# Folding the tokens on VectorE behind the transpose instead of on TensorE before it, in a kernel of linear attention and a gated long convolution

## The chip, the cores and the metric

The kernel runs on one core of one Trainium2 chip. The metric is the device time of one execution in microseconds (us). PE is TensorE, DVE is VectorE, ACT is ScalarE, POOL is GpSimd and SP is SyncE, which here only issues DMAs.

## The reference, cut to what matters

```python
r = np.maximum(x, 0);  phi(x) = concat([r * cos(theta_s), r * sin(theta_s)])   # theta_s = pi/2 * s / S
kv  = einsum('bhsf,bhsd->bhfd', phi(k), v);   z = sum_s phi(k)
att = einsum('bhsf,bhfd->bhsd', phi(q), kv) / (einsum('bhsf,bhf->bhs', phi(q), z) + 1e-6)
x   = att.transpose(0, 2, 1, 3).reshape(8, 576, 512)
x1, x2, x3 = split(x @ w_proj, 3)                     # w_proj is 512 x 1536
x2_conv = irfft(rfft(x2, axis=1) * rfft(filter, axis=0), n=576, axis=1)
out = (x1 * x2_conv * x3) @ w_out                     # float32, 8 x 576 x 512
```

There are 8 batches, 8 heads, 576 tokens and a head size of 64.

## The kernel before, in words

Everything on the chip is in fp16 but for the sums, which TensorE leaves in PSUM as fp32. A batch goes through these steps; the short names are those of the order written out by hand at L886 to L972.

- `Lq`, `Lk`, `Lv` (L147): GpSimd issues loads that turn fp32 into fp16. The first 512 tokens lie four to a row in 128 rows, the last 64 in the lower half of a fifth tile. Each load is two DMAs.
- `pk` (L499): ten operations make relu(k) times cosine and times sine for the five tiles. `pq` (L513): six make relu(q) and relu(q) times tangent. `va` (L533): copies v.
- `kv` (L549): 40 matmuls of 65 columns. `qt` (L566): q is transposed, for batches 0 and 1 on PE, from batch 2 on by four DMA transposes that SP issues (L570, `DMA_QT = 2`). `num` (L593): 40 matmuls of 65 columns, and on DVE a sum, a reciprocal and a multiplication that write `att`, the attention, with tokens in the partitions.
- `fx` (L622): for each of four blocks of channels, four matmuls of 144 columns (L627) and two of 160 (L633) multiply `att` by tables of a few cosines. They transpose it and fold the 576 tokens, by the symmetries of the transform, in one go. ACT brings the result into SBUF.
- `xt` (L652): one DMA transpose of the whole of `att` (20 blocks of 128 by 128) feeds the gates; batch 0 does it on PE (`xp`).
- `pr` (L669): the folded tokens times the middle third of `w_proj`, 16 matmuls of 512 columns and four that fill 64 of the 128 output rows.
- `dft` (L694): 24 matmuls with 32 stationary columns each, 16 of 512 and 8 of 128 moving columns, in three PSUM units; then on DVE products with the filter's spectrum (L712 to L722).
- `ga`, `gb` (L725): 64 matmuls of 288 columns (L731) make x1 and x3 with channels in the partitions, ACT evicts, and `g` multiplies them.
- `inv` (L755): 24 matmuls back to tokens. `y` (L774): per block of channels two operations undo one fold, two the other, and two multiply by `g`; the last one also gathers the 64 left tokens.
- `out` (L807): 16 matmuls of 512 columns and 8 of 256, an eviction, and stores.

PSUM holds four units of two banks, handed out in turn. Helpers record most DVE operations under two lines: L112 (`tsc`, a tensor and a scalar) and L117 (`tt`, two tensors); ACT evictions stand under L137 (`ev`). Every engine works its own list strictly in the order of the plan, so several batches are interleaved by hand and a waiting instruction holds up all that stands behind it.

Of the kernel before, what the change touches and what calls it, by code (L numbers as in the profile page):

```python
# [13 lines left out]
I32 = mybir.dt.int32  # L14


@with_exitstack
def kernel(
# [17 lines left out]


# [11 lines left out]


# [7 lines left out]
    FX = 65536.0  # L58
    SP_ = NJ * 128
    NM = NC * 128  # L60

    consts = ctx.enter_context(tc.tile_pool(name="consts", bufs=1))
    work = ctx.enter_context(tc.tile_pool(name="work", bufs=1))
    psum = ctx.enter_context(tc.tile_pool(name="psum", bufs=4, space=bass.MemoryType.PSUM))
    setup_stack = ExitStack()
    setupp = setup_stack.enter_context(tc.tile_pool(name="setupp", bufs=1))
    late = {}

    def unit(name):
        return psum.tile([128, 2, 512], FP32, tag="u", bufs=4, name=name)  # L70

    def const(name, shape, dt=FP32):
        return consts.tile(shape, dt, tag=name, name=name)

    ccol = const("ccol", [128, NJ])
    scol = const("scol", [128, NJ])
    tcol = const("tcol", [128, NJ])
    epsc = const("epsc", [128, NJ])
    ident = const("ident", [128, 128], FP16)
    half_pi = const("half_pi", [128, 1])  # L80
    m_half_pi = const("m_half_pi", [128, 1])
    m_pi = const("m_pi", [128, 1])
    m_half = const("m_half", [128, 1])
    wr_col = const("wr_col", [128, 1])
    fm = const("fm", [128, 9, 16], FP16)
    fme = const("fme", [128, 4, 5, 16], FP16)
    fcos = const("fcos", [128, 288], FP16)
    fsin = const("fsin", [128, 288], FP16)
    itab = const("itab", [128, 6, QS], FP16)
    itl = const("itl", [128, NC, 2, 2, QS], FP16)  # L90
    hE = const("hE", [128, 2, DM], FP16)
    hO = const("hO", [128, 2, DM], FP16)
    hL = const("hL", [128, 3, 128], FP16)
    wp16 = const("wp16", [128, NC, 3 * DM], FP16)
    wo16 = const("wo16", [128, NC, DM], FP16)
    warm = setupp.tile([128, 512], FP16, tag="warm", name="warm")
    filt16 = setupp.tile([NP, 2, 3 * DM], FP16, tag="filt16", name="filt16")
    feo = setupp.tile([NP, 2, 3, DM], FP16, tag="feo", name="feo")
    k32, v32 = (
        work.tile([128, 4, NJ * D], FP32, tag="att", bufs=2, name=f"{x}32") for x in "kv"  # L100
    )
    qpt_buf = const("qpt", [128, NH, SP_], FP16)
    va_buf = [const(f"va{i}", [128, NH, NJ, 66], FP16) for i in range(2)]
    raw_buf = [const(f"raw{i}", [128, NH, NJ * D], FP16) for i in range(6)]

    last_dve = [None]

# [14 lines left out]
    def rnd(out, in0, mul, add):  # L122

        tsc(out, in0, mul, AL.mult, add, AL.add)
        tsc(out, out, RC, AL.add, -RC, AL.add)

    cc = {}
    mark = {}

    which = [""]  # L130
# [8 lines left out]
    raw_t = {}  # L139
    DMA_QT = 2  # L140
    HALF = (slice(0, 4), slice(4, 8), slice(0, 8))
    held = [None]

    def at(half):
        return HALF[half]

    def load_rows(queue, rw, src, b, hs):  # L147
        to = slice(0, rw.shape[1]) if rw.shape[1] < NH else hs
        first = queue.dma_start(  # L149
            out=rw[:, to, 0 : 4 * D],  # L150
            in_=src[b, hs, 0:NM].rearrange("h (p j) d -> p h (j d)", j=4),
        )
        if held[0] is not None:
            tc.add_manual_dep(
                first.ins, held[0].ins.name,
                mybir.DependencyInfo(mybir.DependencyClass.Sync, mybir.DependencyReason.DATA),
                reason="hold",
            )
        queue.dma_start(
            out=rw[0:64, to, 4 * D : 5 * D], in_=src[b, hs, NM:S].rearrange("h p d -> p h d")  # L160
        )

    def step_load(nm):
        def load(b, half):
            raw_t[(b, nm)] = raw_buf[(3 * b + "qkv".index(nm)) % len(raw_buf)]
            load_rows(nc.gpsimd, raw_t[(b, nm)], {"q": q, "k": k, "v": v}[nm], b, at(half))
            yield
        return load
# [7 lines left out]
    def step_wp(w):  # L176
        nc.gpsimd.dma_start(
            out=wp16[:, :, ds(w * DM, DM)],
            in_=moe_w_proj.rearrange("(i p) n -> p i n", p=128)[:, :, ds(w * DM, DM)],
        )  # L180

        yield

    def step_filt():
        for x in range(2):
            nc.gpsimd.dma_start(
                out=filt16[:, x],
                in_=moe_filter_fft[ds(x * HS, HS)].rearrange("(p j) n -> p (j n)", j=3),
            )
            yield  # L190

    def step_wo():
        nc.gpsimd.dma_start(out=wo16, in_=moe_w_out.rearrange("(i p) n -> p i n", p=128))
        yield

# [5 lines left out]
    def step_iota(part):  # L201
        if part == 0:
            iota("s4_i", [128, NJ], lambda t: [
                (t[:, 0:4], [[1, 4]], 0, 4), (t[0:64, 4:5], [[1, 1]], NM, 1),
                (t[64:128, 4:5], [[1, 1]], 0, 1),
            ])
            yield
            return
        if part == 1:
            iota("p_i", [128, 1], lambda t: [(t, [[1, 1]], 0, 1)])  # L210
            iota("kr_i", [128, 4, 2], lambda t: [(t, [[1, 4], [0, 2]], 1, 0)])
            iota("nrow_i", [128, 128], lambda t: [(t, [[1, 128]], 0, 0)])
            iota("er_i", [128, 4, 16], lambda t: [(t, [[1, 4], [4, 16]], 0, 0)])
            yield
            return
        iota("fr_i", [128, 320], lambda t: [
            (t[:, 0:32], [[9, 2], [18, 16]], 0, 0),
            (t[:, 0:1], [[1, 1]], HS, 0),
            (t[:, 32:160], [[2, 2], [-8, 2], [18, 32]], 10 - HS, 0),
            (t[:, 160:288], [[2, 2], [10, 2], [18, 32]], 1 - HS, 0),  # L220
            (t[:, 288:320], [[9, 2], [18, 16]], 0, 0),
        ])
        iota("s3_i", [128, 3], lambda t: [(t, [[1, 3]], 0, 3)])
        iota("sg_i", [128, 32], lambda t: [(t, [[-2, 2], [0, 16]], 1, 0)])
        iota("sr_i", [128, QS], lambda t: [(t, [[2, 2], [8, QS // 2]], 1, 0)])
        yield

    cc["p"], cc["m"] = small("p"), small("m")
# [4 lines left out]

    def step_ones(i):
        nc.vector.memset(va_buf[i][:, :, :, D : D + 2], 1.0 / A1)
        yield

    def step_cols():
        nc.vector.memset(warm, 0.0)
        nc.vector.memset(half_pi, PI / 2.0)  # L240
        for r in (k32, v32):
            nc.vector.memset(r[64:128, :, 4 * D : 5 * D], 0.0)
        yield
# [4 lines left out]
        yield  # L248
        p = cc["p"]
        nc.vector.tensor_copy(out=p, in_=cc["p_i"])  # L250
        yield
        tsc(ident, cc["nrow_i"], p, AL.is_equal)
# [7 lines left out]
        m = cc["m"]  # L260
        rnd(m, p, 1.0 / 16.0, -15.0 / 32.0)
        yield
        lo = small("lo")
        stt(lo, m, -16.0, p)
        yield
        m8 = small("m8")
        tsc(m8, m, 1.0 / 9.0, AL.mult, -8.0 / 9.0, AL.add)
        yield
        ph = small("ph", 8).rearrange("p (k c) -> p k c", c=2)
        tsc(ph, cc["kr_i"], m8, AL.mult)  # L270
        yield
        tsc(ph[:, :, 0], ph[:, :, 0], 0.25, AL.add)
        yield
        rr = small("ph_r", 8).rearrange("p (k c) -> p k c", c=2)
        tsc(rr, ph, RC, AL.add, -RC, AL.add)
        yield
        nc.vector.tensor_tensor(out=ph, in0=ph, in1=rr, op=AL.subtract)
        yield
        coef = small("coef", 9)
        nc.vector.memset(coef[:, 8:9], 1.0)  # L280
        yield
        nc.scalar.activation(
            out=coef[:, 0:8], in_=ph.rearrange("p k c -> p (k c)"), func=AF.Sin, scale=TWO_PI
        )
        yield
        match = small("match", 16)
        tsc(match, cc["nrow_i"][:, 0:16], lo, AL.is_equal)
        yield
        nc.vector.tensor_tensor(
            out=fm,  # L290
            in0=coef.unsqueeze(2).to_broadcast([128, 9, 16]),
            in1=match.unsqueeze(1).to_broadcast([128, 9, 16]),
            op=AL.mult,
        )
        yield
        tsc(fme, cc["er_i"].unsqueeze(2).to_broadcast([128, 4, 5, 16]), p, AL.is_equal)
        yield
        nc.vector.memset(m_half_pi, -PI / 2.0)
        yield
        nc.vector.memset(m_pi, -PI)  # L300
        yield
        nc.vector.memset(m_half, -FX / 2.0)
# [3 lines left out]

# [4 lines left out]
    def sin_of(dst, m):  # L311
        nc.scalar.activation(
# [3 lines left out]
    def cos_of(dst, m):  # L316
        a = setupp.tile([128, 3 * 320], FP32, tag="tg_a", bufs=1, name="tg_a")
        nr, nc_ = dst.shape
        a = a[0:nr, 0:nc_]
# [6 lines left out]
    def step_rows():  # L326

        p, m = cc["p"], cc["m"]
        sgn = cc["sgn"] = setupp.tile([NP, 32], FP32, tag="sgn", name="sgn")
        nc.vector.tensor_copy(out=sgn, in_=cc["sg_i"][0:NP])  # L330
        yield
        kq = small("kq")
        rnd(kq, p, 1.0 / 32.0, -31.0 / 64.0)
        yield
        k2 = small("k2")
        rnd(k2, kq, 0.5, -0.25)
# [470 lines left out]
    def step_out(b, grp, cut=0):  # L807
# [4 lines left out]
        for cs in ((range(NC),), (range(NC - 1), range(NC - 1, NC)))[cut]:  # L812
            for x, t in enumerate(tiles):
# [14 lines left out]
                if cut and t < 4 and cs[0] > 0:  # L828
                    yield
# [175 lines left out]
```

## Time and profile before

| | |
|---|---|
| runs | 242.19, 251.63, 245.29 us; median 245.29 |
| profiled execution, span | 242.5 us |
| mean granted clock of TensorE | 0.961 |

The page of the profiled execution cuts the span into 40 equal slices of 6.06 us. A digit is the busy share of an engine in tenths, and PEclk the granted clock in tenths.

```profile
PE   6077988978999799998859985999999999999990
DVE  5999878995898998949946985499969967949760
ACT  4259998894888587766617790578768877866741
PEclk9679999997999999999979997999999999999998
DMA  6999999989999999999999999959999933260244
```

All engines start early; DVE is full from the second slice, PE from the fourth. PE falls to 5 to 8 in slices 19 to 25, and the clock shows a dip three times after the start. The DMA engines are taken up until late.

### The profile page before, as it was taken

The numbers are of one execution on the slowest core, as the hardware profiler recorded it, in microseconds if no ns is written. First come the engines' busy times: TensorE is split into PE (matmuls) and PEld (weight loads), VectorE is DVE, ScalarE is ACT, GpSimd is POOL, SyncE is SP. The second block draws the span as 40 slices with busy tenths as digits, with TensorE's granted clock in tenths as the row PEclk, the third lists the DMA queues.
The fourth block names the chain that finished last, engine by engine and source line by source line (L and its number), as shares of the span: only waits on it lengthen the run. The fifth ranks groups of instructions, "written<-read, shape, count | busy, mean of one in ns | idle before, by whom it ended". The sixth has DMA issues, their size and how long they took to land.

```text
span 242.5 us, 5900 instructions
## 1 busy us (share of the span) xinstructions
PE 210.4 (87%) x2276; PEld 142.2 (59%) x2276; DVE 193.1 (80%) x657; ACT 168.6 (70%) x268; POOL 46.4 (19%) x75
## 2 busy tenths in 40 slices
PE   6077988978999799998859985999999999999990
PEld 2066776455558467764527653685678567846740
DVE  5999878995898998949946985499969967949760
ACT  4259998894888587766617790578768877866741
POOL 8882252003331042200220070000200000000000
PEclk9679999997999999999979997999999999999998
DMA  6999999989999999999999999959999933260244
GB/s 170 184 187 201 199 197 190 110 132 194 163 174 164 201 145 209 209 194 219 164 186 189 160 186 211 181 118 242 122 140 192 184 108 124 84 122 1 88 151 151
DMA packets 95612, 39.70 MB, mean 164 GB/s; under 512 B 63648, under 2 KB 91296, under 8 KB 95584
## 3 DMA queue, kind: packets, MB, share of 16 engines
q0 software_dynamic: 38464, 16.26, 54.8%
q1 hardware_dynamic: 56752, 22.49, 46.7%
q10 hardware_dynamic: 368, 0.59, 0.7%
q8 instruction: 17, 0.28, 0.5%
q14 instruction: 11, 0.09, 0.1%
HBM read 33.69 MB, written 9.44 MB: 178 GB/s over the span
## 4 chain that ended last, share of the span: by engine, by line
PE 57%; DVE 16%; DMA 14%; ACT 6%; SPq 3%; issue 2%; ACTq 0%; DVEq 0%
PE x L731 21%; PE out L816 10%; PE x L673 9%; DMA qpt<-qp 7%; DMA xt<-att 5%; PE num L599 3%; PE inv L760 3%; PE inv L764 3%; DVE qp L112 3%; DVE att L117 3%; PE kv L556 2%; DVE kp L112 2%; PE fx L627 2%; SPq L570 2%; PE dft L704 2%
## 5 line engine op out<-in xcount | busy, mean ns | idle before, releaser
L731 PE MATMUL x<-xt,wp 128*128 128x288 f16 x512 | 72.3, 289 | 5.0 <-DMA xt<-att 4.3
L731 PEld LDWEIGHTS <-wp 128*128 128x128 f16 x512 | 48.9, 99 | 21.4 <-DMA xt<-att 5.4
L673 PE MATMUL x<-wp,fx 128*128 128x512 f16 (+1 forms) x160 | 34.5, 387 | 0.0
L816 PE MATMUL out<-wo,y 128*128 128x512 f16 x128 | 31.6, 394 | 0.0
L137 ACT CAST x0s<-x 128x576 f16<-128x576 f32 x32 | 20.4, 641 | 13.9 <-PE x L731 12.4
L137 ACT ACTIVATE os<-out 128x1024 f32<-128x1024 f32 (+1 forms) x22 | 17.5, 795 | 17.6 <-PE out L816 15.7
L137 ACT CAST x2s<-x 128x576 f16<-128x576 f32 x32 | 20.4, 642 | 11.2 <-PE x L731 9.8
L117 DVE TENSOR_TENSOR att<-num,rcp 128x640 f16<-128x640 f32 x32 | 25.9, 820 | 0.5
L137 ACT ACTIVATE x2f<-x 128x1024 f16<-128x1024 f32 (+1 forms) x24 | 20.8, 882 | 7.6 <-PE x L673 7.3
L673 PEld LDWEIGHTS <-fx 128*128 128x128 f16 (+1 forms) x160 | 13.5, 101 | 15.6 <-issue 2.4
L117 DVE TENSOR_TENSOR eo<-eq 128x288 f16<-128x288 f16 x64 | 17.4, 297 | 5.4 <-ACT eq L137 5.4
L137 ACT CAST eq<-inv 128x576 f16<-128x576 f32 x32 | 20.1, 649 | 2.0 <-PE inv L764 1.8
L599 PE MATMUL num<-kvs,qpt 128*128 128x65 f16 x320 | 14.8, 198 | 7.2 <-DMA qpt<-qp 6.7
L816 PEld LDWEIGHTS <-y 128*128 128x128 f16 x128 | 12.6, 102 | 13.9 <-issue 2.5
L599 PEld LDWEIGHTS <-qpt 128*128 128x128 f16 x320 | 13.5, 101 | 10.6 <-DMA qpt<-qp 7.3
L149 POOL DMA_DIRECT2D raw<-in_k_dram x8 | 7.0, 878 | 62.7 <-DVE y L117 55.0
L760 PE MATMUL inv<-itab,yf 128*128 128x144 f16 x128 | 18.0, 232 | 0.6 <-DVE yf L117 0.6
L137 ACT CAST fx<-fx 128x576 f16<-128x576 f32 x30 | 18.1, 653 | 0.3 <-PE fx L633 0.2
L137 ACT CAST xf<-dft 128x1024 f16<-128x1024 f32 (+1 forms) x24 | 17.9, 810 | 0.2 <-PE dft L704 0.2
L117 DVE TENSOR_TENSOR y<-eo 128x288 f16<-128x288 f16 x64 | 17.6, 301 | 0.4
L764 PE MATMUL inv<-itl,yf 128*128 128x288 f16 x64 | 17.5, 294 | 0.0
L117 DVE TENSOR_TENSOR yf<-m,m 128x512 f16<-128x512 f16 (+1 forms) x48 | 15.5, 349 | 0.7
(153 smaller groups left out, 375.4 us busy)
## 6 DMA issues: line engine op xcount, KB each, us to landing
out_dram<-os SPq DMA_DIRECT2D x30, 256.0 KB, 4.6
raw<-in_v_dram POOLq DMA_DIRECT2D x7, 512.0 KB, 8.4
raw<-in_q_dram POOLq DMA_DIRECT2D x7, 512.0 KB, 10.0
raw<-in_k_dram POOLq DMA_DIRECT2D x7, 512.0 KB, 8.6
wp<-in_moe_w_proj_dram POOLq DMA_DIRECT2D x3, 512.0 KB, 11.3
out_dram<-os SPq DMA_DIRECT2D x15, 64.0 KB, 2.3
filt<-in_moe_filter_fft_dram POOLq DMA_DIRECT2D x2, 288.0 KB, 13.8
k<-in_k_dram SPq DMA_DIRECT2D x1, 512.0 KB, 3.9
```

The costliest lines, as they stand in the source:

```text
L112: last_dve[0] = nc.vector.tensor_scalar(out=out, in0=in0, scalar1=s1, scalar2=s2, op0=op0, **({"op1": op1} if op1 else {}))
L117: last_dve[0] = nc.vector.tensor_tensor(out=out, in0=in0, in1=in1, op=op)
L137: return nc.scalar.copy(out=out, in_=in_) if mul is None else nc.scalar.mul(out=out, in_=in_, mul=mul)
L149: first = queue.dma_start(out=rw[:, to, 0 : 4 * D], in_=src[b, hs, 0:NM].rearrange("h (p j) d -> p h (j d)", j=4),)
L556: nc.tensor.matmul(u[:, g, ds((h % 4) * 65, 65)], kp[:, j, h].rearrange("p a b -> p (a b)"), va[:, h, j, 0:65], start=(j == 0), stop=(j == ...
L570: nc.sync.dma_start_transpose(out=qpt[:, hsl].rearrange("p h (j n) -> p (h j) n", j=NJ), in_=qp[:, hsl].rearrange("p h j a b -> p (h j a b)"),
L599: nc.tensor.matmul(u[:, hh, ds(t * 65, 65)], qpt_buf[:, h, ds(t * 128, 128)], kvs[:, h // 4, ds((h % 4) * 65, 65)], start=True, stop=True,)
L673: nc.tensor.matmul(dst, fx[:, c, ds(128 * ch, n)], wp16[:, c, ds(DM, DM)], start=(c == cs[0]), stop=(c == cs[-1]),)
L731: nc.tensor.matmul(u[:, hf, 0:HS], wp16[:, i, ds(w * DM + c * 128, 128)], xt[:, i, ds(HS * hf, HS)], start=(i == 0), stop=(i == NC - 1),)
L760: nc.tensor.matmul(u[:, comp, ds(par * QS, QS)], yf[par][:, comp, ds(c * 128, 128)], itab[:, par + 4 * comp], start=(par == 0), stop=False,)
L764: nc.tensor.matmul(u[:, comp, 0:HS], yf[2][:, comp], itl[:, c, comp].rearrange("p a b -> p (a b)"), start=False, stop=True,)
L816: nc.tensor.matmul(u[:, x], y[:, c, ds(QS * t, 128)], wo16[:, c], start=(c == 0), stop=(c == NC - 1),)
```

## The change

The loads deal the tokens nine to a row: row p holds tokens 9p to 9p+4 in the lower 64 partitions and 9p+5 to 9p+8 in the upper 64, with zeros in the upper half of the fifth tile. So the two halves of a tile hold mirrored residues, and the fold becomes an addition and a subtraction of a tile's first half with another's second half read backwards.

`fx` is gone. `bf` takes its place: eight additions and subtractions on DVE, on `xt`, the transposed attention. The DFT is four matmuls with 128 stationary columns (`dm`), four with 64 rows that add the left tokens (`dr`), and 24 with 32 columns and 128 moving ones (`dl`).

```diff
-    DMA_QT = 2
+    DMA_QT = 1
...
+        rows = src[b, hs].rearrange("h (p j) d -> p h (j d)", j=9)
+        first = queue.dma_start(out=rw[0:64, to], in_=rows[:, :, 0 : NJ * D])
...
+        queue.dma_start(out=rw[64:128, to, 0 : 4 * D], in_=rows[:, :, NJ * D : 9 * D])
...
+    def step_bf(b, x):
...
+        for x_, op in ((0, AL.add), (1, AL.subtract)):
+            tt(
+                out=eo_buf[:, cs, x_, 0:256].rearrange("p c (t n) -> p c t n", t=4),
+                in0=a[:, :, :, 0], in1=a[:, :, ::-1, 1, ::-1], op=op,
+            )
+            yield
+        for x_, op in ((0, AL.add), (1, AL.subtract)):
+            tt(
+                out=eo_buf[:, cs, x_, 256:HS], in0=a4[:, :, 0:32], in1=a4[:, :, ::-1][:, :, 0:32],
+                op=op,
+            )
+            yield
...
+    def step_dm(b, bl):
+        u = pu[b, bl] = unit()
+        for comp, tab, cl in ((0, fcos, 2 * bl), (1, fsin, 2 * bl + 1)):
+            nc.tensor.matmul(
+                u[:, comp], tab[:, ds(128 * bl + 32 * comp, 128)], x2f[:, cl],
+                start=True, stop=False,
+            )
+        yield
+
+    def step_dr(b):
+        for bl in range(2):
+            for s_ in range(2):
+                comp = (s_, 1 - s_)[bl]
+                rows = ds(64 * s_, 64)
+                nc.tensor.matmul(
+                    pu[b, bl][:, comp], flo[rows, bl], x2f[rows, 4], start=False, stop=True,
+                )
+        yield
```

The second half of `bf` folds the results once more, again with four operations (main part and left part, sum and difference). Beyond that:

- `pk` makes relu(k) in one operation over all five tiles and relu(k) times tangent in five; the cosine goes onto v instead (`va`, five operations in place of four copies).
- `xt` is two DMA transposes of 10 blocks; `qt` of batch 1 goes by DMA too. Each gate's eight matmuls stand in the plan as two groups of four.
- `y` works on two blocks of channels at a time (one, for the last batch); left tokens are separate small operations, and one multiplication by `g` covers all 576 tokens. `pd` merges the left part of the products with the second main part.
- Buffers are fixed by name, and a string `UNITS` says which of the four PSUM units each use takes.
- The order of every engine's list is new, and more evictions of the first batches go to DVE, while parts of `pk`, `pq` and `va` go to ACT throughout.

By the built lists, PE goes from 2,276 matmuls to 2,140, DVE from 657 operations to 618 and ACT from 270 to 254; SP issues 42 transposes where it issued 31.

## Prediction

> **What bounds the kernel now.** I read the busy times of the page first, then the shares of the chain of waits, then a stretch of that chain in order of time, then the waits and the stages.
>
> ```profile
> PE 210.4 (87%) x2276; PEld 142.2 (59%) x2276; DVE 193.1 (80%) x657; ACT 168.6 (70%) x268; POOL 46.4 (19%) x75
> ...
> PE 57%; DVE 16%; DMA 14%; ACT 6%; SPq 3%; issue 2%; ACTq 0%; DVEq 0%
> ```
>
> PE is the busiest engine and holds over half of the chain, but DVE is only 17 us behind it: whatever moves from PE to DVE soon meets a second bound. The next view is a stretch of the chain in which nothing but PE stands (start, duration, what), and it gives PE's pace, which the busy time hides because matmuls overlap.
>
> ```profile
> 158.45 0.98 PE x L731 x8
> 159.43 0.25 PE fx L627 x4
> 159.68 0.14 PE fx L633 x2
> ...
> 165.23 3.45 PE x L673 x16
> 168.68 0.98 PE x L731 x8
> 169.66 0.55 PE x L673 x4
> 170.22 1.09 PE dft L704 x24
> ```
>
> A matmul of 512 columns costs 216 ns (3.45 / 16), one block of channels of `fx` 0.39 us, a batch's DFT 1.09. Then the waits (engine, line, releaser: total us, times, longest).
>
> ```profile
> PEld L599 <- DMA qpt<-qp: 7.3, 2, 4.0
> ...
> PE num L599 <- DMA qpt<-qp: 6.7, 2, 3.7
> ...
> PE x L731 <- DMA xt<-att: 4.3, 3, 1.8
> ```
>
> The stages: stretch, length, then busy time (and instructions) of PE, its weight loads, DVE, ACT and POOL, granted clock, DMA share, GB/s.
>
> ```profile
> 80.00:100.00 20.00, 18.35 (x202) 11.79 (x201) 18.98 (x66) 13.27 (x21) 6.36 (x8) 1.00 1.26 193
> ...
> 220.00:242.50 22.50, 16.29 (x120) 9.92 (x117) 13.12 (x44) 10.67 (x20) 0.00 (x0) 0.96 0.31 106
> ```
>
> PE loses 11.0 us to transposes that land late (6.7 + 4.3). From 80 to 100 us DVE is busy 18.98 of 20 (95%), the most that it reaches over a long stretch, and in the last 22.5 it leaves 9.4 idle.
>
> **PE, part by part.** `fx` goes: 4 blocks x 0.39 x 8 batches = -12.5 us. The PE transposes of batch 1 go: the chain has ten of them in 0.68, so 4 x 0.68 = -2.7. The DFT grows. `dm` is four matmuls of 512 columns, 0.86. `dr` is four with 64 rows; no row shows whether two in different rows of the array run side by side, so it lies between 0.43 and 0.86; the nearest row, four DFT matmuls in different columns, runs side by side, and I take 0.43. `dl` is six groups of four small ones: in the old 1.09, four groups of 512 columns take 0.86, which leaves 0.11 for each of its two small groups, so 0.66. Together 1.95 to 2.4 against 1.09: +6.9 (to +10.3) over eight batches. `pr`'s left part is two groups of four instead of two pairs, the same 0.55. Gates, `inv`, `out`, `kv` and `num` keep their matmuls. PE's sum is -12.5 - 2.7 + 6.9 = -8.3 (-4.9 at the dear end of `dr`).
>
> [...]
>
> **DVE.** I take busy time over count from the groups, since neighbours overlap: 0.65 us for 1,024 fp16 elements of two tensors (10.4 / 16), 0.40 for 512 (12.8 / 32), 0.45 for 576, 0.27 for 256, 0.20 for 128 (3.2 / 16), and some 0.17 to 0.25 below that.
> - `bf`: batches 1 to 7 have four of 1,024 and four of 128, 3.4 us each; batch 0 does halves, some 4.6. Together +28.4. The backward reads have no row as inputs; `y`'s backward writes cost the 301 ns of its plain neighbours. [...] I take the pace of the writes.
> - `y`: four groups made 56.2 us (17.4 + 17.6 + 13.3 + 7.9). Now a pair costs four of 512, four of 64 and one of 1,152: 3.1, 14 times, and the last batch's singles 2.2 each: 52.2. So -4.
> - `pd`: 41.1 (20.8 + 4.3 + 12.8 + 3.2) becomes 24 of 1,024, 8 of 1,280, 8 of 256, 16 of 512 and 16 of 640: 38. So -3.
> - `pk`, `pq`, `va`: 55.7 us before. What stays on DVE is 40 of 512 elements with `tcol` and 18 with `ccol` at 0.32 to 0.35, 12 of 2,560 at 0.85, and a few halves: 38. So -17.5.
> - Evictions moved over from ACT: some six of 576 elements at 0.75, three of 1,024 and two of 512 (no row; 0.75 scaled by elements, 1.2 and 0.7), the rest small: +10. Fewer table steps: -3.
>
> DVE's sum is 193.1 + 28.4 - 4 - 3 - 17.5 + 10 - 3 = 204.
>
> **ACT.** `fx`'s evictions go (-18.1). Scaled operations arrive: 47 of 512 elements and a few of 256. The nearest rows are 541 ns for 288 elements with a column of scales and 498 for 256, so about 0.73 for 512: +39, less the copies of v and the old `kp` of 13.6. With evictions handed to DVE and PSUM copies of q's transposes that go, some -12, it comes to 164. ACT stays third.
>
> **Which end is late.** PE alone gives 242.5 - 8.3 = 234.2. DVE at 204 with the share that the bounding engine had before (87%) gives 234.5, and its floor is lower: 204 plus the 3.1 and 9.4 idle at the two ends and 5% of the middle makes 227. The two engines become level, so I take 234 and no more.
>
> **Queues and waits.** The fold stands in DVE's list and waits for the landing of the second half of `xt`; behind it stand `pk`, `pq`, the reciprocals of `num` and `pd` of other batches, and who waits for those is PE, through PSUM units. By the built list, the DVE work between the last write of `att` and the first fold is 5.4, 7.9, 4.5, 7.6, 7.5, 8.9 and 3.3 us for batches 1 to 7. The whole `xt` landed in 6.1 (4.9 to 7.5), a `qpt` of 10 blocks in 3.8 (3.4 to 10.1). At 6.1 only batches 1, 3 and 7 are uncovered, 0.7 + 1.6 + 2.8 = 5 us of DVE's idle, which the share above already has room for. On SP 24 + 7 transposes become 28 + 14; their issue took 24 x 1.42 + 7 x 3.23 = 57 us of the span, and four more at 1.42 lie beside all else. POOL's loads move 640 and 512 bytes per piece where they moved 512 and 128, with a third fewer pieces: no cost. The startup has about as much DVE work as before up to the first gate; 2 us either way.
>
> **The rivals.**
> 1. *The folds wait for late transposes (slower).* For: `num` already waited 3.7 us for a transpose while loads ran, and such landings reached 10.1. If every `xt` took 10.1, the uncovered time is 4.7 + 2.2 + 5.6 + 2.5 + 2.6 + 1.2 + 6.8 = 25.6: 260 us. Against: no whole `xt` took over 7.5, which leaves 2.1 + 3.0 + 4.2 = 9.3, or 243. It decides from about 16 us uncovered, 2.3 per batch. The granted clock falls with such a wait, 0.91 between 111 and 129 us, where PE waited 2.99. [...]
> 2. *DVE becomes the bound, with backward reads at half pace.* [...] For: DVE is already full early. Against: backward writes were not slow.
> 3. *The new order also fills the stalls.* Without the 11.0 us of late transposes: 223. For: `xt` in halves lets a gate start on the first. Against: batch 1 now waits for DMA too.
> 4. *`fx` was hidden.* Its matmuls ran where PE would have waited anyway, and the end stays at 242. Against: the chain has them.
>
> **How the numbers follow.** The sum is made against the span of 242.5; the fastest run shown is 0.3 below it, the median 2.8 above, so I put 1 us on 234. Chances: forecast 0.42 (228 to 241), rival 3 0.20, rival 2 0.15, rival 4 0.06, rival 1 0.17. Within 2% of 245.29 (240.4 to 250.2) is about what a measurement can tell from no change. Faster by more: 0.42 + 0.20, less a little for the upper end, 0.61. Within: 0.21. Slower: rival 1 and a tail of 2, 0.18. The range from 222 to 250 holds rivals 2, 3 and 4 and leaves most of rival 1 outside.
>
> **What would show it.** PE: `dft` near 2 us per batch in the chain, no `fx`, busy near 200. DVE near 204, backward folds at 0.65 us and not 1.2. ACT near 164. DVE's waits for `xt` by DMA below 6 us in all. PE and DVE level in the middle stages. I am wrong if DVE is near full while PE has gaps (rival 2), if the folds wait over 16 us for DMA (1), or if PE's waits for `qpt` are gone (3).

## The result, and the profile after

| | before | after |
|---|---|---|
| median of the runs | 243.74 us (241.3 to 251.63, 4 runs) | 394.73 us (393.03 to 395.3, 4 runs) |
| profiled execution, span | 242.5 us | 393.2 us |
| mean granted clock of TensorE | 0.961 | 0.776 |

The ratio is 1.633 (95% interval 1.625 to 1.642); this ratio and those below leave out executions that took over 1.5% longer than the fastest of the same kernel, which the medians keep. The forecast was 235 with a range of 222 to 250: the direction was wrong.

First the page of the kernel after: busy times, the slices (9.8 us each now), and the shares of the chain of waits.

```profile
PE 228.0 (58%) x2140; PEld 141.1 (36%) x2140; DVE 209.9 (53%) x618; ACT 164.5 (42%) x252; POOL 41.5 (11%) x78
...
DMA  8999899999997994999729999199951931111111
...
DMA 35%; SPq 21%; PE 20%; DVE 12%; issue 3%; ACT 3%; POOL 1%; DVEq 0%; ACTq 0%
```

No engine got much more to do, and none is the bound: PE fell from 87% to 58% of the span. PE's 228 us are no more work either, since part of it ran at a granted clock of 0.50 (224 to 251 us, for one), where a gate matmul takes 447 ns against 286 at 1.00. DMA and SP's queue hold 56% of the chain, where they held 17%. The last seven slices show the DMA engines at a tenth: something still runs there, on few of the engines.

Next its waits (engine, line, releaser: total us, times, longest).

```profile
PEld L670 <- DMA qpt<-qp: 64.9, 9, 12.6
PE ps L670 <- DMA qpt<-qp: 61.1, 7, 12.2
...
ACT os L253 <- DMA out_dram<-os: 32.7, 3, 16.2
...
PE ps L837 <- DMA xt<-att: 26.2, 4, 15.5
```

PE waits 87.3 us for transposes (61.1 + 26.2) where it waited 11.0. ACT's line is the one that gives the clue: an eviction waits until a store has freed its buffer, 16.2 us long. The end of the chain says the same (start, duration, what).

```profile
353.39 22.16 DMA out_dram<-os
```

A store of 256 KB took 22.16 us to land. At the 53 GB/s of the next view 256 KB are 5 us of work (an estimate), so it stood behind other stores. Last, two stretches by windows (length, then busy time and count of PE, its weight loads, DVE, ACT and POOL, granted clock, DMA share, GB/s), with PE long done:

```profile
354.00:375.00 21.00, 0.00 (x0) 0.00 (x0) 1.18 (x3) 0.77 (x2) 0.00 (x0) 0.50 0.14 53
375.00:393.00 18.00, 0.00 (x0) 0.00 (x0) 0.42 (x1) 0.38 (x1) 0.00 (x0) 0.50 0.15 54
```

Only stores are in flight there. The DMA share is 0.14 and 2 of 16 is 0.125: about what two of the 16 DMA engines make that are always busy, at 53 GB/s. In the kernel before the last 6.5 us had a share of 0.47 and 156 GB/s.

What the diff changed there is one line of `out` that neither the excerpt of the change nor the prediction speaks of. With tokens dealt nine to a row, a tile holds token j of each row in its lower half and token j + 5 in its upper, and the store follows that:

```diff
-        ov = out[b, 0:NM].rearrange("(i t) n -> t i n", t=4)      # a store: 128 rows of 512
+        rows = out[b].rearrange("(p j) n -> j p n", j=9)
+        ov = [rows[t : t + 6 : 5] for t in range(4)]               # a store: 2 x 64 rows of 512
```

The bytes, the rows of 2 KB and the number of stores are the same; the outermost dimension went from 128 to 2. That a store with an outermost size of 2 runs on two engines was a guess from this size and the share of 0.14 in the window; e1 to e4 were run to try it.

### The profile page after: what moved, and what is told of

Its sections match the earlier page's. It is cut to its first block, busy times and chain, and to the rows that moved or that the text cites. A ratio compares the mean times of both kernels' runs of the same rounds, so it can differ in the third digit from the quotient of the medians.

```text
span 393.2 us, 5622 instructions
## 1 busy us (share of the span) xinstructions
PE 228.0 (58%) x2140; PEld 141.1 (36%) x2140; DVE 209.9 (53%) x618; ACT 164.5 (42%) x252; POOL 41.5 (11%) x78
## 4 chain that ended last, share of the span: by engine, by line
DMA 35%; SPq 21%; PE 20%; DVE 12%; issue 3%; ACT 3%; POOL 1%; DVEq 0%; ACTq 0%
DMA qpt<-qp 16%; SPq L647 11%; PE ps L837 7%; DMA xt<-att 7%; DMA out_dram<-os 6%; SPq L956 5%; DMA raw<-in_q_dram 4%; PE ps L750 3%; PE ps L924 3%; SPq L692 3%; DVE kp L234 2%; DMA raw<-in_v_dram 2%; SPq L946 1%; PE ps L670 1%; DMA att<-in_k_dram 1%
## 5 line engine op out<-in xcount | busy, mean ns | idle before, releaser
L837 PE MATMUL ps<-xt,wp 128*128 128x288 f16 x512 | 79.0, 305 | 33.6 <-DMA xt<-att 26.2
L670 PE MATMUL ps<-kvs,qpt 128*128 128x65 f16 x320 | 18.3, 217 | 63.5 <-DMA qpt<-qp 61.1
L750 PE MATMUL ps<-wp,fo 128*128 128x512 f16 x128 | 35.2, 415 | 1.1 <-DVE fo L239 0.7
L924 PE MATMUL ps<-wo,y 128*128 128x512 f16 x128 | 34.4, 415 | 0.0
L253 ACT ACTIVATE x2f<-ps 128x1024 f16<-128x1024 f32 (+1 forms) x21 | 18.5, 898 | 24.5 <-PE ps L750 19.7
L253 ACT CAST x2s<-ps 128x576 f16<-128x576 f32 x31 | 19.6, 640 | 19.6 <-PE ps L837 16.6
L870 PE MATMUL ps<-itab,yf 128*128 128x144 f16 x128 | 20.5, 254 | 11.5 <-ACT os L253 11.3
L239 DVE TENSOR_TENSOR att<-ps,rcp 128x640 f16<-128x640 f32 x32 | 26.0, 821 | 0.5
L253 ACT CAST eq<-ps 128x576 f16<-128x576 f32 x31 | 19.3, 646 | 16.2 <-PE ps L874 16.0
L239 DVE TENSOR_TENSOR eo<-xt 128x1024 f16<-128x1024 f16 (+3 forms) x36 | 13.6, 418 | 12.3 <-DMA xt<-att 11.2
L874 PE MATMUL ps<-itl,yf 128*128 128x288 f16 x64 | 20.1, 329 | 0.0
```

The source lines that it names most:

```text
L239: last_dve[0] = nc.vector.tensor_tensor(out=out, in0=in0, in1=in1, op=op)
L253: return nc.scalar.copy(out=out, in_=in_) if mul is None else nc.scalar.mul(out=out, in_=in_, mul=mul)
L670: nc.tensor.matmul(u[:, hh, ds(t * 65, 65)], qpt[:, h, ds(t * 128, 128)], kvs[:, h // 4, ds((h % 4) * 65, 65)], start=True, stop=True,)
L750: nc.tensor.matmul(u[:, x], fo[:, bl, c, x], wp[c], start=(c == 0), stop=(c == NC - 1),)
L837: nc.tensor.matmul(u[:, hf, 0:HS], wp16[:, i, ds(w * DM + c * 128, 128)], xt[:, i, ds(HS * hf, HS)], start=(i == 0), stop=(i == NC - 1),)
L870: nc.tensor.matmul(u[:, comp, ds(par * QS, QS)], yf[:, comp, ds(par * DM + c * 128, 128)], itab[:, par + 4 * comp], start=(par == 0), stop ...
```

## The experiments

All times are medians, with the ratio to runs of the kernel before on the same chip and its 95% interval; those runs of before had medians from 241.8 to 247.4.

**e1: each store cut into halves.** Nothing else differs from the kernel after.

```diff
-                nc.sync.dma_start(out=ov[tiles[i]], in_=os_[:, i])
+                for x in range(2):
+                    nc.sync.dma_start(out=ov[tiles[i]][x], in_=os_[ds(64 * x, 64), i])
```

> Each store of 128 rows is cut into two of 64 rows; the same bytes go to the same places, with 60 issues in place of 30. Theory S (a store whose destination is 2 x 64 rows is worked off by two DMA engines, and the transposes queue behind it there): the stores spread over all engines, the end after the last matmul shrinks from 47 us to under 10, the waits of num for qpt (61 us) fall to about the 7 of before, and the time falls to 225 to 245 us. Theory W (the folds behind the transposes are what is slow, and the stores cost only the 40 us at the end): 345 to 360 us, waits for qpt and xt in the middle unchanged.

Measured: 253.44 us, 1.018 (0.993 to 1.043). Theory S holds in the main: 141 of the 151 us are gone, though 253 is above its 225 to 245. The chain of e1, and then its waits for transposes:

```profile
PE 29%; DMA 29%; DVE 18%; SPq 8%; ACT 7%; issue 5%; POOL 2%; DVEq 0%; ACTq 0%
```

```profile
PEld L670 <- DMA qpt<-qp: 14.7, 7, 6.3
PE ps L670 <- DMA qpt<-qp: 12.1, 4, 6.0
PE ps L837 <- DMA xt<-att: 4.8, 5, 2.1
```

The transposes, which the edit does not touch, come back to 16.9 us of PE's waits from 87.3. So the late transposes were an effect of the slow stores. But e1 is not at 234 either.

How a store holds a transpose up can be read in the kernel after. Its chain has a transpose of q's that lands 14.81 us after SP began to issue it, and two windows lie within that wait:

```profile
299.77 14.81 DMA qpt<-qp
```

```profile
307.00:313.00 6.00, 0.00 (x0) 0.00 (x0) 0.00 (x0) 0.00 (x0) 0.00 (x0) 0.69 0.13 51
313.00:314.50 1.50, 0.00 (x0) 0.00 (x0) 0.00 (x0) 0.00 (x0) 0.00 (x0) 0.50 1.17 241
```

Up to 313 us the DMA engines move 51 GB/s, the rate of stores alone, and then 241. By the packet records of the trace 148 packets of stores and 8 of transposes start in the first window, the last of the stores ends at 312.95, and from 313.0 to 314.6 it is 1,524 of transposes and none of stores. So this transpose all but stood still beside a store. Why the whole of it did, and not only a part on two engines, stays open. SP itself was held up too: to issue a transpose of q's took it 2.99 us by the median and at most 10.67, against 1.42 and 3.52 in the kernel before and 1.49 and 2.33 in e1.

**e2: the kernel before with the stores of the kernel after.** The rows of the output stand elsewhere, those of the left tokens too (a line not shown); all else is the kernel before.

```diff
-        ov = out[b, 0:NM].rearrange("(i t) n -> t i n", t=4)
+        rows = out[b].rearrange("(p j) n -> j p n", j=9)
+        ov = [rows[t : t + 6 : 5] for t in range(4)]
```

> The kernel before, with the stores' destinations written as the changed kernel writes them (2 x 64 rows for a tile, and the fifth tile to the row it has there), so that rows of the output stand elsewhere; nothing else is changed. Theory S: the stores alone carry the loss, 340 to 400 us, with long waits for transposes. Theory W: the kernel before has no folds behind transposes, so only its end grows: 265 to 285 us.

Measured: 369.81 us, 1.504 (1.474 to 1.534). The store alone costs the kernel before half of its time again, with the old folds, the old order and the old loads.

```profile
ACT os L137 <- DMA out_dram<-os: 51.8, 4, 18.4
...
PE x L731 <- DMA xt<-att: 29.3, 7, 10.4
```

These waits of e2 are those of the kernel after: evictions for a store, gates for a transpose.

**e3 and e4: the outermost size as the dose.** The kernel after with stores of 4 x 32 and 8 x 16 rows; the rows of the output stand elsewhere, those of the left tokens too (a line not shown).

```diff
-        ov = [rows[t : t + 6 : 5] for t in range(4)]
+        ov = [rows[t // 2 : t // 2 + 7 : 2, ds(32 * (t % 2), 32)] for t in range(4)]   # e3
+        ov = [rows[0:8, ds(16 * t, 16)] for t in range(4)]                             # e4
```

> The changed kernel with each store's destination as 4 x 32 rows; rows of the output stand elsewhere. Theory S in its form that the outermost size is the number of engines: four engines, the DMA share after the last matmul doubles from 0.14 to about 0.27, the end halves from 47 to some 24 us, and the whole is 265 to 310 us. If only one shape or the other is slow, and not the outermost size: near 393 or near 235.

> The same with 8 x 16 rows; rows of the output stand elsewhere. Theory S: eight engines, DMA share in the end about 0.5, the whole 235 to 260 us, at most 20 above the kernel with whole spread. Theory W: 350 us.

Measured: 315.82 us (1.284, 1.258 to 1.311) and 269.84 (1.097, 1.076 to 1.118). Both lie above what theory S gave, 265 to 310 and 235 to 260. Windows behind the last matmul, of e3 and then of e4, show the number of engines more directly:

```profile
294.00:306.00 12.00, 0.00 (x0) 0.00 (x0) 1.61 (x4) 1.15 (x3) 0.00 (x0) 0.50 0.29 102
```

```profile
258.00:262.00 4.00, 0.00 (x0) 0.00 (x0) 1.18 (x3) 0.43 (x2) 0.00 (x0) 0.61 0.52 184
```

At outermost sizes of 2, 4 and 8 the DMA share is 0.14, 0.29 and 0.52 (2, 4 and 8 of 16 are 0.125, 0.25 and 0.5), at 53, 102 and 184 GB/s, and by the packet records of the kernel after 2.1 packets of stores are in flight at a time (307 to 313 us). At these three sizes the share is about that of as many engines as the outermost size.

Against 252 with stores of 64 rows (e5 below), sizes of 2, 4 and 8 cost 143, 64 and 18 us. If the time of the stores goes as one over the number of engines k, and stores of 64 rows run on 16 (an assumption that no window shows), the cost over 16 engines goes as 1/k - 1/16, and the three give 326, 340 and 285 us for it: nearly one constant. The last is the least certain, since the runs of e5 lie 4 us apart. An estimate from the window of the kernel after agrees: 32 stores of 256 KB are 8.39 MB, at 53 GB/s that is 158 us on two engines and, by the same assumption, an eighth of it, 20, on sixteen, so 138 us more.

**e5: two tiles in one store of half the partitions.** As many stores as in the kernel after, of 64 rows in runs of 4 KB; only the last batch's tiles are stored in halves, as in e1.

```diff
-            for i in range(2):
-                nc.sync.dma_start(out=ov[tiles[i]], in_=os_[:, i])
+            both = out[b].rearrange("(p j) n -> p j n", j=9)
+            for x in range(2):
+                nc.sync.dma_start(
+                    out=both[:, 5 * x + tiles[0] : 5 * x + tiles[0] + 2], in_=os_[ds(64 * x, 64)]
+                )
```

> The kernel after, with the stores of two tiles cut the other way: not one store for each tile (2 x 64 rows of 2 KB), but one for each half of the partitions, with both tiles in it (64 rows of 2 tiles, 4 KB that lie together in memory). As many stores as in the kernel after, where the halved stores of e1 were twice as many; the last batch's four tiles keep halves, dealt to SP and ACT. Theory S (all of the 150 us was the outermost size of 2): it stands with e1, at 244 to 253 us. A second theory, that e1 still lost time to SP issuing twice as many stores (some 28 more at 0.6 us, and 10.2 us from the last matmul to the end against 7.3 in the kernel before): 3 to 6 us under e1, most of it behind the last matmul. Should it stand over 300 us, the outermost size is not what decides.

Measured: 252.05 us, 1.039 (1.007 to 1.071), as e1 within the intervals. The number of stores made no difference that can be told. The runs from here on ask why this kernel stands at 250 and not at the forecast 234.

**e6 and e7: no loads of batches 4 to 7,** in e5 and in the kernel before. These batches compute on what the buffers hold.

```diff
     def step_load(nm):
         def load(b, half):
+            if b >= 4:
+                yield
+                return
```

> e5 without the loads of q, k and v of batches 4 to 7 (those batches compute on what the buffers hold). What is left of the gap between e1 (252.4 us profiled) and the forecast (234): theory L says that loads and DMA transposes of the same stretch hold each other up. In e1 the loads of batch 6 were issued at 138 us, between the four transposes of batch 5 at 132 to 138, and those of batch 7 at 166 to 169, with the transposes of batch 6 at 161 to 167, and the chain waits 11.6 and 12.8 us for a transpose in these two places. By L this kernel is 12 to 20 us under e5, 228 to 238, and no transpose behind 110 us takes over 6 us. Theory F (folds wait for xt) and theory V (VectorE is the bound, 210 us busy) both say that loads are not what ends last: within 5 us of e5.

> The kernel before without the loads of batches 4 to 7. Theory L, that the collision belongs to the new order: the kernel before waits for transposes some 14 us in all, in pieces of up to 4, so it gains 2 to 6 us and stands at 237 to 243. If it gains as much as e6 does on e5 (12 us or more), loads cost both kernels alike, and L does not explain what is left between the kernel with spread stores and the kernel before.

Measured: 242.85 us (239.4 and 246.29) and 233.98 (233.56 and 234.4). By medians the loads cost e5 some 9 us and the kernel before some 11; by the lowest runs 9 (from 248.49) and 6 (from 239.72). That is under the 12 to 20 that theory L gave for e5, and over the 5 that F and V left room for. So theory L as it was put falls: that the loads weigh more on the new order is not shown, and without them it is still 6 to 9 us behind.

**e8: folds that wait for no transpose.** They read `att` in place of `xt`, so they fold other values.

```diff
-        xt = xt_buf[b % 2]
+        xt = att_buf[b % 2].rearrange("p c t n -> p c (t n)")
```

> e5 with the folds reading att, not its transpose xt (the folded values are other ones): the transposes are still made, and TensorE's gate projections still read them, but no fold waits for one. Rival 1 of the prediction, in a milder form (theory F): the folds wait for the transposes and pass it on, so this kernel is over 5 us under e5. Theory L: the folds stand far enough behind the transposes, and it is within 3 us of e5.

Measured: 258.9 us, 7 above e5. No gain, so nothing speaks for theory F; but the run is not clean, since `att` is now read later and its buffer comes free later.

**e9 and e10: VectorE in the set-up.** e9 leaves out the folds of batches 0 and 1, which then use zeros and what stands in the buffer; e10 moves five operations of batch 0 from VectorE to ScalarE in the plan (`gb:0.3`, `ga:0.2`, `ga:0.3`, `xe:0.0`, `ti`) and leaves nothing out.

> e5 without the folds of batches 0 and 1 (fo and fl of batch 0 are zeros that GpSimd writes, batch 1 uses what stands there). Theory V, VectorE bounds the set-up: in e5 the first inverse matmul starts at 63.9 us, in the kernel before at 51.6, and VectorE is busy for 58 of these 64 us; from the first inverse to the last, e5 takes 168.0 us and the kernel before 171.9, so the whole loss stands ahead of 64 us. The folds of batch 0 are some 3.7 us of VectorE between 26 and 37 us, those of batch 1 about as much between 61 and 68. By V the first inverse comes 3 to 6 us earlier and the end 4 to 8 us (243 to 247 profiled). By theory L (loads and transposes alone make what is left) nothing of this matters: within 2 us of e5's 250.9.

> e5 with five evictions and table pieces of batch 0 moved from VectorE to ScalarE (x2s 0.67, twice x0s 0.75, xf 1.21, a table piece 0.4: 3.8 us of VectorE between 36 and 50 us); nothing is left out. ScalarE is busy for 10.0 and 13.2 of 20 us there. By V: 2 to 5 us under e5. By L: within 2 us. Should ScalarE's slower order cost as much as VectorE gains, it also stands within 2 us, but with the first inverse no earlier.

Measured: 255.16 us for e9 (1.055, 1.040 to 1.070) and 252.51 for e10 (1.043, 1.031 to 1.054). Neither gains. In e9 the first gate stood 3.5 us later than in e5, which I did not account for, so e9 says less than it was meant to. In e10 the first inverse matmul came 2.0 us earlier, and by the second batch's 1.4 us later. Theory V falls as an account of the end.

**e11 and e12: loads earlier.** e11 puts `Lv:6.2 Lk:6.2` behind `va:5.2'v`, and `~Lq:7.2 Lk:7.2 Lv:7.2` ahead of `xt:5.1`; e12 is e10 and e11 together.

> e5 with the loads of v and k of batch 6 right behind that of q (124 us in place of 138), and all three of batch 7 ahead of the transposes of batch 5's tokens (150 in place of 166); nothing is left out. Leaving the loads of batches 4 to 7 out gave e6 7 us over e5 by the profiled spans, but gave the kernel before 10. If it is the moment of these loads that costs, this kernel gains 3 to 7 us; if it is the loads as such, whenever they run, it gains under 2.

> e10 and e11 together. By V and the moment of the loads: the sum of their gains, 5 to 10 us under e5, so 241 to 246 and level with the kernel before or a little ahead of it. If set-up and loads hide each other, no more than the better of the two.

Measured: 261.91 us (1.079, 1.063 to 1.095) and 262.05 (1.081, 1.069 to 1.093): 10 us lost where 3 to 7 were to be gained. The chain of e11, in the stretch that changed:

```profile
126.43 11.22 DMA xt<-att
...
138.58 9.91 DMA qpt<-qp
```

The loads left one group of transposes and met another. In e5 the same kind of line stands at the old place:

```profile
164.55 12.86 DMA qpt<-qp
...
177.46 0.64 PE ps L670 x10
```

The median landing in e1 is 3.8 us for `qpt` and 5.4 for `xt`; these three, beside loads, took 9.9 to 12.9.

**e13 and e14: loads later,** behind the transposes: e13 puts `~Lv:6.2 Lk:6.2` behind `num:5.0*3` and `~Lq:7.2 Lk:7.2` behind the third `num:6.1`, with the first `pq:7.2` and `pk:7.2` moved back; e14 does the second part alone.

> e5 with the loads later in place of earlier: v and k of batch 6 wait until the third group of num of batch 5 has read its transposes (some 144 us in place of 138.7), q and k of batch 7 until the second group of batch 6 has (some 170 in place of 163.5), with the first pq and pk of batch 7 moved behind them; nothing is left out. Theory M (a load hurts when it is issued while transposes are under way: the transpose of 164.6 us landed 12.9 us later in e5, against a median of 3.8; and e11, which issued the loads just ahead of other transposes, lost 10 us): 3 to 7 us under e5, and no transpose behind 130 us takes over 7 us. If loads cost the same wherever they stand, or if the later loads only put a wait on VectorE in the place of the one taken away, it is within 2 us of e5 or above it.

> e5 with the loads of batch 7 alone later (170 us in place of 163.5). By M: 2 to 5 us under e5 and 1 to 3 above e13. If the whole gain of e13 is here, the loads of batch 6 do no harm where they stand.

Measured: 251.5 us (1.042, 1.027 to 1.057) and 255.19 (1.036, 1.022 to 1.050), whose four runs lie from 247.85 to 261.11. No gain over e5. Yet the mechanism of theory M is there: PE's waits for `qpt` fell to 2.5 us in e13. The chain of e14 shows where they went:

```profile
165.41 0.67 POOL raw L263
166.08 10.56 DMA raw<-in_k_dram
...
176.72 0.04 ACT kp L586
```

The load itself is now what ScalarE waits for, and evictions stand behind it. One wait took the place of the other. Of the kernels that leave nothing out, none beats the kernel before.

**What is left, and what stays open.** The windows of the kernel before, and then of e5, hold the difference of the two:

```profile
0.00:20.00 20.00, 10.66 (x112) 7.13 (x112) 16.84 (x92) 10.08 (x16) 15.91 (x37) 0.83 1.19 182
20.00:40.00 20.00, 16.57 (x206) 13.41 (x207) 17.30 (x49) 18.31 (x34) 7.40 (x9) 1.00 1.43 197
40.00:60.00 20.00, 17.58 (x234) 10.52 (x233) 17.08 (x54) 15.56 (x27) 2.34 (x3) 0.91 1.05 149
...
160.00:180.00 20.00, 20.00 (x222) 13.59 (x218) 17.47 (x60) 15.73 (x25) 1.56 (x2) 1.00 0.94 146
```

```profile
0.00:20.00 20.00, 12.28 (x95) 7.59 (x96) 15.84 (x68) 11.46 (x22) 13.32 (x38) 0.83 1.12 183
20.00:40.00 20.00, 17.61 (x139) 12.03 (x138) 17.24 (x58) 10.04 (x15) 3.77 (x6) 0.74 1.05 163
40.00:60.00 20.00, 13.14 (x212) 8.05 (x210) 18.10 (x47) 13.21 (x21) 2.74 (x4) 0.87 1.09 166
...
160.00:180.00 20.00, 13.35 (x146) 8.29 (x145) 11.91 (x36) 6.98 (x12) 4.09 (x6) 0.85 1.20 188
```

Busy time times granted clock, summed over all such windows, is an estimate of PE's work at full speed (the clock of a window covers its idle time too): 204 us before, 199 in e5. So the work did fall, by 5 us. But e5 loses 12.1 us to the clock (211.1 - 199) where the kernel before loses 6.4, and is idle for 39.8 (250.9 - 211.1) where the other is for 32.1. By 60 us it has done 34.7 us of work against 41.4, and from 160 to 180 it does 11.3 against 20. The second place is a transpose that lands late beside loads, by the chain above (12.86 us). For the first, folds and evictions were tried without a gain, and the cause stays open.

## Why the prediction was wrong, point by point

- **PE, part by part: right in kind.** `fx` is gone, and the DFT is in the chain of the kernel after at its pace: 0.86 for `dm`, 0.54 for `dr` (taken 0.43, bounds 0.43 and 0.86), 0.45 for `dl` (0.66), in all 1.85 against 1.95:

```profile
255.96 0.86 PE ps L772 x4
256.82 0.45 PE ps L793 x24
257.27 0.54 PE ps L783 x4
```

Four 64-row matmuls in 0.54, under the 0.86 of four one after the other: two in different rows of the array do run side by side. For the 0.11 over two steps of 216 ns no run shows a cause. The 8.3 us of less work measure some 5 by the windows.
- **DVE: right.** 209.9 against 204. Backward reads (`eo` from `xt`) cost 685 ns for 1,024 elements, beside 682 for the forward ones: the same pace, as taken.

```profile
L239 DVE TENSOR_TENSOR eo<-xt 128x1024 f16<-128x1024 f16 x14 | 9.3, 685 | 11.2 <-DMA xt<-att 11.2
```

Mis-sized was relu(k) over 2,560 elements, 1.474 us against 0.85, 4 us in all.
- **ACT: right.** 164.5 against 164; 512 elements with a column of scales took 0.72 (0.73).
- **"Queues and waits": this is the step that failed.** It counted SP's transposes from 31 to 42 and found the extra ones beside all else, and it costed the loads. It left out what else SP issues, the stores, whose pattern the diff changed: a term of nothing, for which no reason was given. Moved and changed DMAs were to be counted one by one; this one was worth 143 us (394.7 against 252.1 in e5), 17 times the 8.3 of PE's sum. None of the prediction's three signs of being wrong came true, since none of them looks at a store.
- **POOL's loads, "no cost": not refuted.** Without the loads of batches 4 to 7 both kernels gain, 9 us and 6 to 11.
- **"Which end is late":** the share of 87% for the bounding engine was carried over from the old order. With the stores mended it is 84% (211.1 of 250.9), PE running slower at that. By the windows 7.7 us more idle time, 5.7 more lost to the clock and 3.3 less work saved make the 16.7 between e5's span of 250.9 and the 234.2 of PE's sum.
- **The rivals.** Rival 1 named late transposes as the slower outcome, and late they were. But it put them into the folds' wait and bounded them by landings of the kernel before, at most 10.1 us; the folds waited 11.2 us in all, PE 87.3. The cause of the lateness was in no rival. Rival 2 is out, since no run shows backward reads at half pace (685 ns beside 682), and rival 3 too, since the stalls grew. Rival 4 is not settled: with stores of 64 rows (e5) the work fell by 5 us and the idle time rose by 8, as if `fx` had been hidden, but the end came 8 us later and not level.

## What to carry to other kernels

For every DMA that a change touches, stores too, write down both access patterns and look at the size of the outermost dimension: a layout that is free for the engines can shrink it from 128 to 2, and the count of bytes, rows and DMAs shows nothing. Here it showed in the profile as a DMA share of 0.14 with only stores in flight, and as long waits for other DMAs (87.3 us of PE's for transposes). Cut such a store so that the partitions come first (here: one store per half with two tiles in it, 252.1 us in place of 394.7).

## What the runs showed of the hardware

- Time against outermost size k of the stores: 394.7 us at 2, 315.8 at 4, 269.8 at 8, 252.1 at 64; the time above the last, over 1/k - 1/16, is 326, 340 and 285 us.
- Where only stores ran, the DMA share was 0.14, 0.29 and 0.52 at outermost sizes of 2, 4 and 8: about 2, 4 and 8 engines of 16.
- In these windows the stores moved 53, 102 and 184 GB/s.
- A transpose of q's that lands in 3.8 us by the median (before, e1) took 9.9 (e11) and 12.9 (e5) beside loads. In the kernel after one all but stood still for 6 us beside a store (51 GB/s, then 241). The longest two on its chain took 17.2 and 16.7 us; beside the second no store of 2 KB rows was in flight, only loads and, from 120.6 us, a store of 64 rows of 1 KB.
- SP's issue of a transpose of q's grew from a median of 1.42 us to 2.99, and to 10.67 at most, in the kernel after; in e1, with stores of 64 rows, it was 1.49 and 2.33.
- The granted clock is 0.50 in the two long windows behind the last matmul of the kernel after and from 224 to 251 us, where PE is busy for 10.0 of 27 us; it is 0.74 to 0.87 in the first 60 us of e5, where PE is idle for 17.0. The mean is 0.961 before and 0.776 after.
- A gate matmul of 288 columns takes 447 ns at a granted clock of 0.50 and 286 at 1.00; its mean is 289 before and 305 after.
